# A transformer block on one core: a list scheduler's order against an order written out, operation by operation

## The chip, the cores and the metric

The kernel runs on one core of a Trainium2 chip. Times are device microseconds (us) from the first to the last instruction of an execution, with what lies around it. The kernel before took 836.15 us, the median of three runs (835.84 to 837.64). TensorE (PE in the profile) multiplies matrices, VectorE (DVE) does element-wise work and reductions, ScalarE (ACT) does copies, casts and activations, GpSimd (POOL) a little of the rest, and SyncE (SP) issues nearly all transfers. PEld is the loading of weights into PE, which runs beside its multiplications.

## The reference, cut to what matters

```python
S, D, H, Dh, W, dil, F = 2048, 640, 32, 20, 8, 2, 1728        # all float32, B = 1
def _A_ref(x, wqkv, wo):                                       # attention
    qkv = (x @ wqkv).reshape(B, S, 3, H, Dh) ...               # q, k, v
    idx = pos[:, None] - (arange(W) * dil)[None, :]            # 8 keys: s, s-2, ..., s-14
    logits = einsum("bhsd,bhswd->bhsw", q, k[idx]) * Dh ** -0.5   # masked where idx < 0
    attn = softmax(logits)
    o = einsum("bhsw,bhswd->bhsd", attn, v[idx])
    return o.reshape(B, S, D) @ wo
def _B_ref(x, w_gate, w_up, w_down):                           # feed-forward
    return (silu(x @ w_gate) * (x @ w_up)) @ w_down

h  = x + _A_ref(_layernorm(x), wqkv, wo)
h2 = h + _B_ref(_layernorm(h), w_gate, w_up, w_down)           # the output
```

## The kernel before

Each fp32 matrix product is made of three products of rounded parts: a high part times a high part, a low part times a high part and a high part times a low part. The high part is a cast (on ACT: L506 and L606 for activations, L617 and L939 for weights), the low part the difference between the value and its high part (on DVE: L507, L607, L619, L956). So each tile of activations and of weights goes through ACT and then DVE before PE has all three products.

The sequence is cut into four batches of 512 rows, each of four row groups of 128, and the 640 columns of Q, K and V into four groups of eight heads. For a batch the kernel loads x (L577 row by row for the first batch, L568 in one transfer for another), takes the layer norm on ACT (L382, L389), turns rows into columns (L604 and L504 on PE, or L512, a 128x2560 transpose on DVE), multiplies by the weight tiles of wqkv (loaded by L616, 128x480 each; products L643) and stores Q, K and V in DRAM. The local attention is element-wise work on DVE alone: products with shifted K (L692) and V (L727), sums (L699, L735), maximum and softmax (L710, L711), L765 turns results. Then come the product with wo (L890, evicted by L893), the residual (L901), the second layer norm (L496, L504 to L507 make its columns, high and low part), the products with w_gate and w_up (L962, L1046, L1068), the gating (L986 to L997) and the product with w_down (L973, L1093, L1103, L1298). A part of the feed-forward of the last batches is computed in a form that needs fewer products, by sums and differences of rows: L1204 makes differences of weights, L1207 their low parts, L1223 evicts a product bank into a sum, L1250 multiplies the two halves. That stage runs from about 654 to 766 us and is called the pair stage below. Eight banks of 512 columns take the products, so PE also waits for whoever empties a bank.

The whole program is recorded first: P.add notes the engine, a cost, the tiles read and written and a function for each of 2846 operations. `order()` then puts all of them in one sequence, and each engine's instructions are issued in that sequence. An engine works through its own queue in order: an instruction whose input is not there holds up all that stand behind it on that engine. Before, the sequence comes from a list scheduler (`listed`), which takes the ready operation with the earliest due time; `latest` computes due times backwards from the order of the PE work; nine ROUNDS repeat both with other parameters; and SHIFT moves some 370 operations by hand-set amounts. The costs in P.add, `nb` and HOP are the scheduler's alone.

## Time and profile before

| what | value |
| --- | --- |
| median of the timed runs | 836.15 us (835.84 to 837.64) |
| the profiled execution: span from first to last instruction | 835.3 us |
| PE busy | 826.3 us (99%), 4061 matmuls |
| DVE busy | 755.7 us (90%), 916 instructions |
| ACT busy | 421.3 us (50%), 740 instructions |
| POOL busy | 23.1 us (3%) |
| granted TensorE clock, mean | 0.999 of full speed |
| moved by DMA | 211.08 MB, 253 GB/s on the mean |

The page gives no other time for the profiled execution than its span; the median of the runs is 0.85 us above it. A share of busy time is a mean over the whole span, so the windows below give it by stage. In a timeline, a number in square brackets is the time in which the engine sat idle before the row, and the name behind the arrow is the instruction that ended it. In the chain of waits, "x60" says that 60 instructions of one line ran one behind the other; what they take beyond 60 times the time of one is waiting.

### The profile page before, as it was taken

To read this page: it belongs to the slowest core of one execution; us is meant where nothing else is said; L and a number is where in the kernel's file an instruction comes from. 1 tells how busy PE (TensorE), PEld (TensorE's weight loads), DVE (VectorE), ACT (ScalarE), POOL (GpSimd) and SP (SyncE) were. 2 spreads that over 40 slices of the span, in tenths; PEclk is the share of its full clock that TensorE was granted. 3 is DMA by queue.
4 is the path that set the end of the run, shared out by engine and by line. 5 is a ranking of instruction groups with operands and counts; after the bars stand their busy time and mean duration, and the time that the engine had idled before them with its cause. 6 is when DMAs were issued, how large, how long until landed. Compare 5 with 4: busy or idle time off the path is not lost.

```text
span 835.3 us, 11299 instructions
## 1 busy us (share of the span) xinstructions
PE 826.3 (99%) x4061; PEld 712.8 (85%) x4061; DVE 755.7 (90%) x916; ACT 421.3 (50%) x740; POOL 23.1 (3%) x34
## 2 busy tenths in 40 slices
PE   8999999999999999999999999999999999999998
PEld 6888888889978888887888888888988888888998
DVE  7599999999999999999999999998869888777982
ACT  7856473333783435654543476565695323323440
POOL 0000000000100000001000000000000000000000
PEclk9999999999999999999999999999999999999999
DMA  8897868568679764899899758899999634457722
GB/s 274 288 348 275 267 213 283 185 207 308 186 219 343 257 197 177 326 303 349 282 313 349 271 173 315 255 288 352 352 339 320 224 115 151 124 175 258 273 99 75
DMA packets 113223, 211.08 MB, mean 253 GB/s; under 512 B 37952, under 2 KB 70400, under 8 KB 112528
## 3 DMA queue, kind: packets, MB, share of 16 engines
q1 hardware_dynamic: 112864, 209.96, 74.0%
q8 instruction: 32, 0.52, 0.2%
q10 hardware_dynamic: 304, 0.41, 0.1%
q14 instruction: 23, 0.19, 0.1%
HBM read 151.27 MB, written 59.05 MB: 252 GB/s over the span
## 4 chain that ended last, share of the span: by engine, by line
PE 84%; DVE 8%; ACT 3%; DMA 3%; issue 1%; SPq 0%; POOL 0%; DVEq 0%; ACTq 0%; POOLq 0%
PE bank L962 22%; PE bank L1046 18%; PE bank L643 15%; PE bank L973 10%; PE bank L1298 7%; PE bank L890 6%; DMA fa<-in_x_dram 2%; PE bank L1103 1%; DVE fa L692 1%; PE bank L1093 1%; DVE fa L735 1%; PE bank L1068 1%; DVE fa L727 1%; DVE fa L699 1%; ACT ra L617 1%
## 5 line engine op out<-in xcount | busy, mean ns | idle before, releaser
L962 PE MATMUL bank<-shb,ra 128*128 128x512 f32 x810 | 190.0, 390 | 1.3 <-DVE shb L507 1.3
L962 PEld LDWEIGHTS bank<-shb,ra 128*128 128x128 f32 x810 | 151.4, 188 | 32.7 <-ACT shb L506 1.5
L643 PE MATMUL bank<-ra,sha 128*128 128x480 f32 x480 | 105.2, 379 | 0.2 <-ACT ra L617 0.2
L643 PE MATMUL bank<-ra,shb 128*128 128x480 f32 x470 | 102.5, 378 | 0.0
L643 PEld LDWEIGHTS bank<-ra,sha 128*128 128x128 f32 x480 | 89.8, 188 | 14.5 <-ACT ra L617 0.6
L643 PEld LDWEIGHTS bank<-ra,shb 128*128 128x128 f32 x470 | 88.1, 188 | 13.2
L692 DVE TENSOR_TENSOR fa<-fa 128x2560 f32<-128x2560 f32 x32 | 90.2, 2820 | 0.9 <-DMA fa<-qsc 0.4
L727 DVE TENSOR_TENSOR fa<-fa 128x2560 f32<-128x2560 f32 x32 | 90.3, 2822 | 0.8
L699 DVE TENSOR_REDUCE fa<-fa 128x128 f32<-128x2560 f32 x32 | 89.9, 2810 | 0.4
L1046 PE MATMUL bank<-shb,ra 128*128 128x512 f32 x360 | 89.4, 395 | 0.6 <-DVE fa L990 0.6
L973 PE MATMUL bank<-ra,acts 128*128 128x512 f32 x328 | 80.7, 391 | 0.0
L1046 PEld LDWEIGHTS bank<-shb,ra 128*128 128x128 f32 x360 | 66.0, 188 | 16.2 <-DVE fa L1223 1.7
L735 DVE TENSOR_TENSOR fa<-fa 128x1280 f32<-128x1280 f32 (+2 forms) x70 | 76.7, 1096 | 1.3
L890 PE MATMUL bank<-ra 128*128 128x320 f32 x480 | 74.1, 310 | 0.0
L890 PEld LDWEIGHTS bank<-ra 128*128 128x128 f32 x480 | 71.7, 188 | 2.4 <-ACT fa L893 1.0
L648 ACT ACTIVATE st<-bank,fa 128x480 f32<-128x480 f32 x64 | 41.0, 656 | 64.1 <-PE bank L643 59.5
L973 PEld LDWEIGHTS bank<-ra,acts 128*128 128x128 f32 x328 | 61.1, 188 | 13.2 <-DVE acts L997 0.5
L1046 PE MATMUL bank<-ra 128*128 128x512 f32 x288 | 69.1, 390 | 0.0
L1046 PEld LDWEIGHTS bank<-ra 128*128 128x128 f32 x288 | 53.9, 188 | 11.1
L1223 DVE TENSOR_TENSOR fa<-bank,fa 128x512 f32<-128x512 f32 x60 | 41.0, 689 | 19.8 <-PE bank L1046 19.0
L939 ACT CAST ra<-fa 128x1280 fp32r<-128x1280 f32 (+1 forms) x38 | 45.6, 1207 | 22.9 <-PE bank L962 12.3
L996 ACT CAST acts<-fa 128x512 fp32r<-128x512 f32 x34 | 21.0, 620 | 48.7 <-DVE fa L986 47.0
(189 smaller groups left out, 1059.8 us busy)
## 6 DMA issues: line engine op xcount, KB each, us to landing
fa<-in_ffn_dram SPq DMA_DIRECT2D x28, 960.0 KB, 6.4
fa<-ksc SPq DMA_DIRECT2D x16, 880.0 KB, 5.4
fa<-vsc SPq DMA_DIRECT2D x16, 880.0 KB, 7.3
ra<-lsc SPq DMA_DIRECT2D x21, 640.0 KB, 5.8
ra<-lsc SPq DMA_DIRECT2D x27, 320.0 KB, 3.7
lsc<-ra SPq DMA_DIRECT2D x13, 640.0 KB, 4.6
fa<-in_ffn_dram SPq DMA_DIRECT2D x12, 640.0 KB, 4.0
ra<-tsc SPq DMA_DIRECT2D x8, 960.0 KB, 7.1
```

Source lines behind the costliest of these rows:

```text
L643: T.matmul(banks[bk][:, 0:480], l, r_(wq(g, w, c), 480), start=(p, c) == first_mm, stop=(p, c) == last_mm)
L648: P.add("ACT", act(480) + 0.06, lambda bk=bk, j=j: A.activation(stage_t()[:, so : so + 1920].rearrange("p (t j c) -> p t j c", t=3, j=NJ)[ ...
L692: P.add("DVE", dve(2560), lambda: V.tensor_tensor(f(PROD, 2560).rearrange("p (j w c) -> p j w c", j=2, w=W), window(ko, 2 * jp), f(qo + 32 ...
L699: P.add("DVE", dve(2560), lambda: V.tensor_reduce(f(lo + 128 * jp, 128), f(PROD, 2560).rearrange("p (n d) -> p n d", d=DH), axis=AX.X, op= ...
L727: V.tensor_tensor(f(PROD, 2560).rearrange("p (j w d) -> p j w d", j=2, d=DH), bass.AP(tensor=fa[:, vo : vo + 160].tensor, offset=fa[:, vo ...
L735: V.tensor_add(dst(v), v[:, :, 0:m, :], v[:, :, m : 2 * m, :])
L890: T.matmul(banks[bk][:, 0:320], l, r_(m, 320), start=p == 0 and c == 0, stop=p == 2 and c == NC - 1)
L939: P.add("ACT", act(n), lambda: A.copy(r_(gu, n), f(raw, n)), r=[rf(raw, n)], w=[rr(gu, n)], prio=PR["fh"])
L962: T.matmul(banks[bk], r_(gu + 1280 * w + wid * c + col, 128), x2(a, c), start=p == 0 and c == 0, stop=p == 2 and c == NC - 1)
L973: T.matmul(banks[bk][:, lo:hi], l, m, start=first and p == 0, stop=last and p == len(passes) - 1)
L1046: T.matmul(banks[bk], r_(ws[w] + 256 * q, 128), x(a, c), start=start and p == n == q == 0, stop=stop and p == 2 and n == len(terms) - 1 an ...
L1298: T.matmul(banks[bks[j]][:, 0:320], t(a, 128, 128 * j), r_(ws[w], 320), start=p == q == 0, stop=p == NP - 1 and q == 2)
```

## The change

The list scheduler with its parameters and its SHIFT table goes. In its place stands ORDER, a tuple of all 2846 operation numbers, and `order()` emits the operations by their place in it (an operation comes only after those it depends on). The operations, what they read and write, their shapes and their dependences stay the same; only the sequence differs. Lines of the kernel after are higher by 12 (L604 becomes L616, L616 becomes L628, L1223 becomes L1235).

```diff
-LANES, HOP = 8, 0.035
-LAP = {"PE": 0.0, "ACT": 0.1, "DVE": 0.08, "POOL": 0.0, "SP": 0.0}
-ROUNDS = ((1.1, 3, 3.5), (1.5, 6, 1.5), (1.4, 20, 3.5), ...
-SHIFT = {
-    7: 3.5, 9: -106.8, 22: 0.4, 31: -515.8, 32: -221.5, 33: -238.8, 34: -84.5, 35: -34.6, 36: -483.8, 37:
...
+ORDER = (
+    3, 0, 6, 11, 42, 10, 9, 2, 31, 7, 32, 33, 15, 8, 36, 37, 34, 12, 13, 39, 43, 40, 16, 17, 1, 47, 41, 118, 119, 19,
...
     def order(self):
-        start = self.listed()
-        for stretch, serial, dma in ROUNDS:
-            start = self.listed(self.latest(start, stretch, dma), serial)
...
-        key = [(t + SHIFT.get(n, 0.0), n) for n, t in enumerate(start)]
-        heap, out = [key[n] for n in range(len(ops)) if not left[n]], []
+        place = {n: i for i, n in enumerate(ORDER)}
+        heap, out = [(place.get(n, n), n) for n in range(len(left)) if not left[n]], []
         heapq.heapify(heap)
         while heap:
             n = heapq.heappop(heap)[1]
             out.append(n)
...
-    def latest(self, start, stretch, dma):
...
-    def listed(self, last=None, serial=0.0):
...
```

Of the operations, 642 of PE's 808 stand at another place in its queue than before (164 by more than five places), 753 of DVE's 855 (183 by more than five), 492 of ACT's 579 (100) and 536 of SP's 586 (201, at most 84 places). POOL's 18 stay. Three places follow.

The queue of SP at the start of the program, before: in_x is the first batch's rows (64x640 and 128x640) and the second batch (128x2560), in_wqkv the weight tiles.

```order
L572 DMA fa<-in_x_dram 64x640
L577 DMA fa<-in_x_dram 128x1x640 x3
L616 DMA fa<-in_wqkv_dram 128x480 x8
L349 DMA ksc<-fa 8x1120
L349 DMA vsc<-fa 8x1120
L1411 DMA fa<-in_const_dram 128x1x32
L616 DMA fa<-in_wqkv_dram 128x480 x8
L568 DMA fa<-in_x_dram 128x1x2560
L616 DMA fa<-in_wqkv_dram 128x480 x2
```

The same queue after:

```order
L584 DMA fa<-in_x_dram 64x640
L589 DMA fa<-in_x_dram 128x1x640
L628 DMA fa<-in_wqkv_dram 128x480 x4
L589 DMA fa<-in_x_dram 128x1x640
L628 DMA fa<-in_wqkv_dram 128x480 x2
L589 DMA fa<-in_x_dram 128x1x640
L628 DMA fa<-in_wqkv_dram 128x480 x2
L361 DMA ksc<-fa 8x1120
L628 DMA fa<-in_wqkv_dram 128x480 x7
L580 DMA fa<-in_x_dram 128x1x2560
L628 DMA fa<-in_wqkv_dram 128x480
```

Four weight tiles now go ahead of the last two row loads of the first batch, and 15 instead of 16 stand ahead of the load of the second batch.

The queue of DVE at the first columns of the second layer norm, before: L507 makes the low part of these columns from a bank (bank_73 is the first that PE reads), L496 low parts that come without a bank, L699 is a reduction of the attention, L956 makes low parts of gate and up weights.

```order
L956 TENSOR_TENSOR ra<-fa,ra 128x640
L496 TENSOR_TENSOR shb<-fa,shb 128x2x128 x2
L699 TENSOR_REDUCE fa<-fa 128x128
L710 TENSOR_REDUCE fa<-fa 128x32
L507 TENSOR_TENSOR shb<-bank_73,shb 128x256
L496 TENSOR_TENSOR shb<-fa,shb 128x2x128
L507 TENSOR_TENSOR shb<-bank_74,shb 128x512
L496 TENSOR_TENSOR shb<-fa,shb 128x2x128
L507 TENSOR_TENSOR shb<-bank_75,shb 128x512
```

The same place after (L777 is L765 of before, L519 is L507, L508 is L496, L711 is L699, L968 is L956):

```order
L777 STREAM_TRANSPOSE fa<-fa 128x2x5x32
L722 TENSOR_REDUCE fa<-fa 128x32
L968 TENSOR_TENSOR ra<-fa,ra 128x640
L711 TENSOR_REDUCE fa<-fa 128x128
L508 TENSOR_TENSOR shb<-fa,shb 128x2x128
L968 TENSOR_TENSOR ra<-fa,ra 128x640
L519 TENSOR_TENSOR shb<-bank_74,shb 128x512
L519 TENSOR_TENSOR shb<-bank_73,shb 128x256
L508 TENSOR_TENSOR shb<-fa,shb 128x2x128 x4
L519 TENSOR_TENSOR shb<-bank_75,shb 128x512
```

The bank of 512 columns is now taken first (PE's first product there is also the one that reads it), a transpose L777 stands ahead, and the L508s stand behind the reduction.

The queue of DVE in the pair stage, before: L1223 empties a bank that PE fills next, L1204 and L1207 prepare weights, L1250 is the gating product.

```order
L1250 TENSOR_TENSOR fa<-fa 128x512
L1204 TENSOR_TENSOR fa<-fa 128x512 x3
L1109 TENSOR_TENSOR fa<-bank_72,fa 128x320
L1223 TENSOR_TENSOR fa<-bank_74,fa 128x512
L1207 TENSOR_TENSOR ra<-fa,ra 128x512
L1223 TENSOR_TENSOR fa<-bank_73,fa 128x512
L1207 TENSOR_TENSOR ra<-fa,ra 128x512
L1204 TENSOR_TENSOR fa<-fa 128x512
```

The same place after (L1235 is L1223 of before, L1216 is L1204, L1219 is L1207, L1262 is L1250, L1121 is L1109):

```order
L1235 TENSOR_TENSOR fa<-bank_73,fa 128x512
L1235 TENSOR_TENSOR fa<-bank_75,fa 128x512
L1216 TENSOR_TENSOR fa<-fa 128x512
L1262 TENSOR_TENSOR fa<-fa 128x512
L1121 TENSOR_TENSOR fa<-bank_72,fa 128x320
L1235 TENSOR_TENSOR fa<-bank_74,fa 128x512
L1235 TENSOR_TENSOR fa<-bank_73,fa 128x512
L1219 TENSOR_TENSOR ra<-fa,ra 128x512
L1262 TENSOR_TENSOR fa<-fa 128x512
L1235 TENSOR_TENSOR fa<-bank_73,fa 128x512
```

The evictions L1235 now stand ahead of differences of weights and low parts that stood ahead of them, and come two together.

## Rows read from the trace of the kernel before

**Rows 1.** the page: busy time, then one group of instructions

```profile
PE 826.3 (99%) x4061; PEld 712.8 (85%) x4061; DVE 755.7 (90%) x916; ACT 421.3 (50%) x740; POOL 23.1 (3%) x34
...
L692 DVE TENSOR_TENSOR fa<-fa 128x2560 f32<-128x2560 f32 x32 | 90.2, 2820 | 0.9 <-DMA fa<-qsc 0.4
```

**Rows 2.** windows: length, busy PE, PEld, DVE, ACT, POOL, PEclk, DMA, GB/s

```profile
12.00:34.00 22.00, 22.00 (x103) 19.04 (x102) 12.01 (x35) 17.98 (x45) 0.00 (x0) 1.00 0.89 291
...
39.00:237.00 198.00, 197.84 (x954) 173.46 (x953) 195.00 (x173) 102.36 (x203) 9.05 (x10) 1.00 0.75 246
237.00:242.00 5.00, 3.62 (x20) 2.83 (x19) 5.00 (x10) 4.98 (x8) 0.00 (x0) 1.00 0.91 298
...
654.00:766.00 112.00, 112.00 (x503) 91.99 (x502) 88.52 (x140) 34.77 (x64) 0.10 (x1) 1.00 0.48 160
```

**Rows 3.** waits of PE: line <- what it waited for: us, times, longest

```profile
PE bank L604 <- DVE sha L607: 1.4, 1, 1.4
...
PE bank L962 <- DVE shb L507: 1.3, 1, 1.3
PE bank L1046 <- DVE fa L990: 0.6, 1, 0.6
```

**Rows 4.** waits of all engines, one row of DVE

```profile
DVE fa L512 <- ACT fa L382: 8.5, 1, 8.5
```

**Rows 5.** chain of waits: start us, us, engine and line, instructions

```profile
17.32 10.49 DMA fa<-in_x_dram
...
45.49 4.64 DMA fa<-in_wqkv_dram
...
256.96 6.80 PE bank L962 x30
...
305.93 2.19 PE bank L890 x15
...
308.81 2.29 PE bank L890 x15
...
390.78 4.88 PE bank L973 x19
...
645.78 1.96 PE bank L1093 x12
...
660.97 1.64 PE bank L1046 x6
...
672.25 13.87 PE bank L1046 x60
...
686.84 42.60 PE bank L1046 x186
...
730.17 35.87 PE bank L1046 x156
```

**Rows 6.** timeline of PE at the start: start us, us, instructions, [idle before]

```profile
8.41 0.66 PE L604 MATMUL bank<-fa 128*128 128x128 f32 x4 [1.40 <-DVE sha L607]
...
10.56 0.47 PE L643 MATMUL bank<-ra,sha 128*128 128x480 f32 x1
```

**Rows 7.** timeline of DVE, 35 to 40 us

```profile
38.01 1.19 DVE L619 TENSOR_TENSOR ra<-fa,ra 128x480 fp32r<-128x480 f32 x2
```

**Rows 8.** timeline of DVE around the first LN2 columns

```profile
235.85 2.81 DVE L699 TENSOR_REDUCE fa<-fa 128x128 f32<-128x2560 f32 x1
...
239.10 0.41 DVE L507 TENSOR_TENSOR shb<-bank,shb 128x256 fp32r<-128x256 f32 x1
239.44 0.41 DVE L496 TENSOR_TENSOR shb<-fa,shb 128x256 fp32r<-128x256 f32 x1
239.77 0.68 DVE L507 TENSOR_TENSOR shb<-bank,shb 128x512 fp32r<-128x512 f32 x1
...
243.44 0.90 DVE L765 STREAM_TRANSPOSE fa<-fa 128x320 f32<-128x320 f32 x2
```

**Rows 9.** line L1207: durations ns min/median/max, first and last start

```profile
L1207 DVE TENSOR_TENSOR ra<-fa,ra x24: 679/682/691, 652.1 to 752.2; 128x512 fp32r<-128x512 f32 x24
```

More of the change, by code (lines that the diff above doesn't have):

```diff
@@ L32 @@
 SCALE = DH ** -0.5
[L35 to L37 removed]
 PR = {'tp': 6, 'mx': 2, 'mh': 2, 'ml': 2, 'mld': 3, 'dt': 2.2, 'g1': 0.6, 'y1': 0.6, 'x': 0.5, 'yst': 8, 'yld': 2, 'wqd': 4, 'wqh': 0.5, 'wql': 4, 'qev': 1, 'kvs': 0.4, 'atl': 1.2, 'exp': 0.5, 'ost': 3, 'wod': 2, 'woh': 8, 'wol': 1.2, 'old': 1.5, 'fld': 4, 'lst': 6, 'wev': 1.5, 'fh': 2.2, 'fl': 8, 'ln1': 8, 't1': 1, 'wo0': 1.2, 'wo': 2.2, 'ln1t': 1.2, 'xb': 0.4, 'tr': 10, 't1t': 2.2, 'ln1d': 0.5, 'hst': 10, 'hld': 10, 'ht': 1, 'hc': 2, 'jd': 3, 'jp': 8, 'js': 4, 'jl': 0.4, 'ja': 0.5, 'jfld': 1.2, 'jfh': 4, 'jfl': 1, 'jhi': 4, 'jmu': 0.4, 'jlo': 0.9, 'jcm': 0.5, 'w3': 1, 'w3e': 8, 'w3o': 0.4, 'w3x': 8, 'w3l': 2.2, 'jy': 6}
[L40 removed]
[34 rows of a table removed]
[L75 removed]
+ORDER = (
[143 rows of a table added]
+)
 class Plan:
@@ L102, in order @@
     def order(self):
-        start = self.listed()
-        for stretch, serial, dma in ROUNDS:
-            start = self.listed(self.latest(start, stretch, dma), serial)
-        self.start, self.end = start, max(t + o[1] for t, o in zip(start, self.ops))
-        ops = self.ops
-        left = [len(o[3]) for o in ops]
-        key = [(t + SHIFT.get(n, 0.0), n) for n, t in enumerate(start)]
-        heap, out = [key[n] for n in range(len(ops)) if not left[n]], []
+        left = [len(o[3]) for o in self.ops]
+        succ = [[] for _ in self.ops]
+        for n, o in enumerate(self.ops):
+            for d in o[3]:
+                succ[d].append(n)
+        place = {n: i for i, n in enumerate(ORDER)}
+        heap, out = [(place.get(n, n), n) for n in range(len(left)) if not left[n]], []
         heapq.heapify(heap)
@@ L114, in order @@
             out.append(n)
-            for m in self.succ[n]:
+            for m in succ[n]:
                 left[m] -= 1
                 if not left[m]:
-                    heapq.heappush(heap, key[m])
+                    heapq.heappush(heap, (place.get(m, m), m))
         return out
-    def latest(self, start, stretch, dma):
-        ops = self.ops
-        t, due = 5.0, {}
-        for n in sorted((n for n, o in enumerate(ops) if o[0] == "PE"), key=lambda n: start[n]):
-            due[n] = t
-            t += ops[n][1]
-        last = [0.0] * len(ops)
-        for n in reversed(range(len(ops))):
-            eng, cost, _, _, prio, _, nbytes = ops[n]
-            if eng == "SP":
-                cost += nbytes + dma
-            elif eng == "DVE" and prio == 20:
-                cost *= stretch
-            last[n] = min(min((last[m] - HOP for m in self.succ[n]), default=1e9) - cost, due.get(n, 1e9))
-        return last
```

76 lines of the change are left out of this document (removed), and 175 rows, old and new, of tables (ORDER, SHIFT).

## The prediction

> **What bounds the kernel now.** I read the busy times first: PE works 826.3 us of a span of 835.3, DVE 755.7 [rows 1]. The reader is to see that an order of the same work can win very little: what PE does not use is 9.0 us, and the rest must come from matmuls that are stretched by waits. Next the windows by stage [rows 2], in which two things stand out. From 39 to 237 us DVE has 195.0 busy of 198.0, the pauses between its instructions included, so it is as full as PE there; from 654 to 766 it has 88.52 of 112.0, so it has 23 us of room. And PE loses 1.38 us in the 5 us from 237 to 242. Then who waits for whom: PE has few long waits, 1.4 at the start for L607, 1.3 at L962 for L507 and 0.6 at L1046 for L990 [rows 3]. The longest of DVE is 8.5 us for L382, before it starts its transpose L512 at 35 us [rows 4]; from there on DVE runs without a rest to the wait of PE at 237. So the place at 237 is bound by DVE, not by PE: time that PE wins before it is lost again there, unless DVE comes earlier too. Last the chain of waits, which gives the stretched groups [rows 5]. The measure for these is an undisturbed group: 30 products of 512 columns in 6.80 us, 0.2267 each, and 15 of 320 columns in 2.19 us, 0.146 each.
>
> **The change part by part.** All operations and their durations stay, so each term below is a wait that goes or comes. The sum is made against the profiled execution's 835.3 us; the median of the runs is 836.15, 0.85 above it, and I carry the differences over to the median.
>
> *Start.* SP issues four weight tiles ahead of the second half of the first batch's rows, and PE's first QKV products stand ahead of most L604, where they fill the wait of 1.40 us and come before the 10.56 us at which the first stands now [rows 6]. The gain lies between 0 and 1.4; I take 0.8, near the middle, since one more warm-up product stands first. Another weight tile that is issued at 45.49 and is waited for until about 50.1 [rows 5] is issued some 20 us earlier; that frees at most 0.7 us, taken as 0.65. These 1.45 us of PE count nothing in the sum, because PE arrives earlier at 237 us and there waits for DVE that much longer. If that cover is gone, they are worth 1.45.
>
> *First columns of the second layer norm (237 us).* Between the L512 at 35 us and the first low part, DVE has more ahead of it after: one more L619 (1.19 for two [rows 7], 0.60), one more L765 (0.90 for two [rows 8], 0.45), and the bank of 512 columns, which PE's first product there reads, takes 0.68 where that of 256 took 0.41 (0.27 more); one L496 stands behind it now (0.33, from 239.44 to 239.77 [rows 8]). Together +0.99. Three more L496 stand ahead of the last low part, which adds 1.38 there in all (0.60 + 0.45 + 0.33), but PE has two groups of five products in front of it (2.27), so the first low part decides. Against it stands the second batch's x: it is loaded in 10.49 us from 17.32 [rows 5], and its layer norm is what L512 waits for. One tile of 128x480 (0.246 MB) fewer goes ahead of it; at 291 GB/s [rows 2] that is 0.84. Of the 0.9 us that L692 waits in all, 0.4 is for a load of Q [rows 1], before 237 us; its store and load stand earlier in SP's queue after, and it goes. Net 0.99 - 0.84 - 0.4, about -0.2. The ends: +0.63 if the load takes its 10.49 us from issue whatever is ahead of it, -0.6 if it gains half as much again. I take the middle since the transfers are busy for 22 us on end there, at 0.89 [rows 2].
>
> On this place the row shows a load of 10.49 us, more than twice what its 1.31 MB need at 291 GB/s (4.5), so it stood behind others or shared with them [rows 2, 5]. The Trainium skill, page "DMA: Bandwidth & Descriptors", section "Queues, rings and completion order", says that the transfers of one issuing engine share its rings, one on each DMA engine, and that each consumes its descriptors in ring order. By that rule a tile less ahead is a tile's time less, the -0.2; by the bare row, with a fixed time from issue to landing, it is +0.63.
>
> *Products with wo.* L890 in one bank waits for its eviction where only 0.68 us of other products lie between two groups: 2.29 instead of 2.19 [rows 5], four times. After, 1.4 us or more lie between, and one new pair is as close as before: -0.3. The ends are -0.4 and 0.
>
> *390 us.* 19 products take 4.88 where 19 x 0.2267 = 4.31 [rows 5], because the low part L997 stands behind an L692 of 2.8 us on DVE. After, it stands ahead of it: of 0.57 I take 0.5; the ends are 0.57 and 0.
>
> *565 us.* PE waits 0.6 for L990 [rows 3], which stands behind a 2.8 us L727 in both orders; one L1374 fewer is between the sums and the L727. Between 0 and 0.6 I take 0.35.
>
> *646 us.* 12 products of 320 columns take 1.96 where 12 x 0.146 = 1.75 [rows 5]: -0.2, the ends -0.2 and 0.
>
> *Pair stage.* PE runs into banks that L1223 has not emptied. The groups take 1.64 for 6 (1.36 undisturbed), 13.87 for 60 (13.60), 42.60 for 186 (42.17) and 35.87 for 156 (35.37) [rows 5]: 0.28 + 0.27 + 0.43 + 0.50 = 1.48. After, the evictions stand 3 to 7 us of DVE work further ahead, in a stage in which DVE has room [rows 2], and with the durations of the trace the least margin between an eviction and the product that fills the bank grows from 0.1 to about 2 us, an estimate. A part of the losses has no releaser in the trace, so I take -1.1; the ends are -1.48 and 0.
>
> *New waits.* Of 808 PE operations 642 change place, and not each can come as well covered as before. No row shows them. I take five of 0.1, the size of the wait at L890 [rows 5], +0.5; the ends are 0 and 1.5 (that of the wait at 237, 1.3, and two small ones).
>
> Sum: -0.2 - 0.3 - 0.5 - 0.35 - 0.2 - 1.1 + 0.5 = -2.15, hence 836.15 - 2.15 = 834.0.
>
> **The rivals.**
>
> *The early gains come through.* The second batch's x lands earlier by 1.4 us more than I take, since the whole start of SP's queue is 64 rows and tiles in another order. Then DVE reaches 237 us earlier by that, PE's 1.45 from the start is worth its time, and the result is 834.0 - 1.4 = 832.6. For it speaks that the load takes 10.49 where its bytes need 4.5; against it, that only one tile goes from ahead of it.
>
> *The gains are given back at DVE.* DVE is as full as PE to 237 us [rows 2], and what PE wins at 390 and at the wo products is lost where it next waits for DVE (565 us, L990 behind the L727, which the new order leaves there). Without the 0.3, 0.5 and 0.35, and without the 0.2 at 237, the sum is -0.2 - 1.1 + 0.5 = -0.8, and the result 835.3.
>
> *Slower, by the pair stage.* The evictions stand ahead of the low parts L1207 now. Each product that reads such a low part waits if it comes late, and nothing behind it on PE can go ahead. Its price is one eviction's place, 0.68 us [rows 9], in each of the six pairs, 4.1 us, and the pair stage wins nothing: 834.0 + 1.1 + 4.1 = 839.2. It decides from four pairs on (1.1 + 2.7 = 3.8, 837.8). For it: the 24 low parts now lie behind evictions that wait for PE, so one late bank holds up both. Against: the narrowest of them has a margin of some 1 us in the trace, and by the durations it grows to more than 3, and DVE has 23 us of room.
>
> That the order is not carried out as written is no rival: the engines' queues after are those of ORDER.
>
> **How the numbers follow.** The forecast of 834.0 has a chance of 0.51, the early gains 0.22, gains given back 0.16, slower 0.11. The forecast's own range is 833.2 to 834.9: from 0.8 less (the full 1.48 and no new waits) to 0.9 more (the term at 237 at +0.63). The range for 8 in 10 goes to 831.8, where the early gains come with no new waits (832.6 - 0.5) and a little of the ends beside, and to 836.6, where the gains are given back and the new waits are 1.5 and not 0.5 (835.3 + 1.0, and 0.3 of the ends). What a measurement of this kernel can tell from no change is about 0.2%, 1.67 us; that lies at 834.5 and 837.8. Of the forecast's 0.51 some 0.36 lies below 834.5, with the early gains 0.58 for faster. Its other 0.15 and 0.16 of the gains given back are 0.31 for the same, and the pair stage's 0.11 is slower.
>
> **What would show it.** In the profile after: the first QKV product at about 8 us; the wait of PE for L507's successor L519 about 1.2 us longer than the 1.3 of now (1.45 that PE is earlier, less 0.2 that DVE is); the load of the second batch's x shorter than 10.49 us; no group of L985, the successor of L973, with 4.88 us for 19 near 390 us; in the pair stage no wait for L1235 and PE at less than 1.0 us above the count times 0.2267. I am wrong if the wait at 237 us is gone (then the early gains came through), if PE still waits for L1235, or if it waits for L1219. A change of DVE's 8.5 us wait by more than 1.5 us would overturn the term at 237.

## The result, and the profile after

The changed kernel took 840.91 us (median of 4 runs, 840.04 to 841.76) against 836.0 for the kernel before (4 runs): ratio 1.0048, interval 1.0034 to 1.0062. It is slower; 834.0 was forecast, with 836.6 as the upper end of the range for 8 in 10. Repeated with 10 runs beside 34 of the kernel before (e0 below), the ratio is 1.0034 (1.0023 to 1.0044), 2.9 us. The span of the profiled execution is 839.5 us, 4.2 above before.

The page's busy times, columns as in [rows 1]:

```profile
PE 827.3 (99%) x4061; PEld 713.1 (85%) x4061; DVE 759.1 (90%) x916; ACT 417.3 (50%) x740; POOL 25.1 (3%) x34
```

DVE works 3.4 us more and POOL 2.0 more with the same 916 and 34 instructions. That is the first sign: the durations were to stay. The windows, columns as in [rows 2]:

```profile
12.00:34.00 22.00, 21.08 (x104) 18.01 (x103) 12.99 (x37) 20.23 (x50) 0.00 (x0) 1.00 0.91 291
...
39.00:237.00 198.00, 197.44 (x952) 173.17 (x950) 194.05 (x172) 98.94 (x197) 9.57 (x10) 1.00 0.74 245
237.00:242.00 5.00, 3.25 (x16) 2.53 (x15) 5.00 (x10) 5.00 (x11) 0.00 (x0) 0.83 0.75 231
394.00:565.00 171.00, 169.56 (x791) 141.69 (x789) 167.13 (x166) 90.29 (x140) 7.97 (x8) 1.00 0.87 291
...
654.00:766.00 112.00, 112.00 (x508) 92.26 (x508) 90.89 (x145) 33.79 (x65) 0.10 (x1) 1.00 0.51 169
```

PE now stands still in places where it did not: 0.92 us in 12:34, 1.75 instead of 1.38 in 237:242, and 1.44 in 394:565. The waits of PE, in the form of [rows 3], some of the rows:

```profile
PE bank L974 <- DVE shb L519: 1.2, 1, 1.2
PE bank L616 <- DVE fa L455: 0.9, 1, 0.9
PE bank L985 <- DVE acts L1004: 0.8, 1, 0.8
PE bank L516 <- ACT fa L489: 0.6, 1, 0.6
PE bank L655 <- ACT st L660: 0.6, 1, 0.6
```

The wait for L519, which was to grow to 2.5, is as long as before, and four new ones stand beside it (the one for L489 is scatter at least in part: 0.64 us of it stand in e9 below, whose order there is the old one). The chain in the pair stage, columns as in [rows 5]:

```profile
680.98 10.70 PE bank L1058 x46
692.41 12.07 PE bank L1058 x53
705.21 58.46 PE bank L1058 x255
```

46, 53 and 255 products would take 10.43, 12.02 and 57.83 undisturbed: 0.27, 0.05 and 0.63 are still lost.

To place the loss, take from a product's start the undisturbed times (0.2268 us for 512 columns, 0.2167 for 480, 0.1467 for 320, 0.109 for 128) of all products ahead of it. What is left, less the same 2.2 us in every row for the first products, is the time PE has lost by then:

| at us | 12 | 34 | 100 | 236 | 245 | 387 | 395 | 500 | 560 | 600 | 650 | 760 | last |
| --- | --- | --- | --- | --- | --- | --- | --- | --- | --- | --- | --- | --- | --- |
| before | 4.21 | 4.20 | 4.68 | 4.29 | 6.18 | 6.47 | 7.08 | 7.45 | 7.64 | 8.83 | 9.49 | 10.99 | 10.99 |
| after | 2.84 | 3.93 | 3.72 | 4.34 | 8.15 | 8.61 | 8.60 | 9.87 | 11.60 | 13.14 | 13.42 | 14.54 | 14.74 |
| e0, after again | 2.93 | 4.05 | 3.84 | 5.00 | 7.58 | 8.04 | 8.03 | 8.55 | 10.53 | 11.80 | 12.09 | 13.23 | 13.42 |

The start wins 1.37 us, and at 236 us nothing is left of it. It was not lost in a longer wait at 237, as forecast, but ahead of it: 1.09 between 12 and 34 us, and 0.6 between 100 and 236. Between 236 and 245 us PE then loses 3.81 (e0: 2.58) where it lost 1.89 before, and between 500 and 560 it loses 1.73 (e0: 1.98) where it lost 0.19. The rest of the 4.2 is the way from the last product to the end, about 0.4 longer. The same start scatters by itself: at 12 us the profiles of this document have lost 2.6 to 5.0 with the start of after and 3.7 to 5.9 with that of before, so 1.37 is one pair's figure. In this execution 8 products from 240.5 us took 0.427 us each (the window's granted clock is 0.83, so part of it at 1.2 and not 2.4 GHz), after PE had stood still for 0.75 and 1.32 us.

**What stood still.** DVE and then POOL of the changed kernel, 100 to 108 us, columns as in [rows 8]:

```profile
100.29 2.83 DVE L704 TENSOR_TENSOR fa<-fa 128x2560 f32<-128x2560 f32 x1
103.53 3.82 DVE L541 TENSOR_TENSOR sha<-fa,sha 128x512 fp32r<-128x512 f32 x4 [0.41 <-ACT sha L540]
107.27 2.81 DVE L711 TENSOR_REDUCE fa<-fa 128x128 f32<-128x2560 f32 x1
```

```profile
103.26 0.20 POOL L765 TENSOR_TENSOR fa<-fa 128x1 f32<-128x1 f32 x1 [26.49 <-DVE fa L704]
103.41 1.58 POOL L767 TENSOR_TENSOR fa<-fa 128x640 f32<-128x640 f32 x1
```

The same place in the kernel before:

```profile
104.08 1.89 DVE L529 TENSOR_TENSOR sha<-fa,sha 128x512 fp32r<-128x512 f32 x3
105.89 2.82 DVE L692 TENSOR_TENSOR fa<-fa 128x2560 f32<-128x2560 f32 x1
108.74 2.82 DVE L699 TENSOR_REDUCE fa<-fa 128x128 f32<-128x2560 f32 x1
```

```profile
109.00 1.57 POOL L755 TENSOR_TENSOR fa<-fa 128x640 f32<-128x640 f32 x1
```

POOL adds attention sums as soon as the product L692 is done (its L765 reads one element of the product). In the kernel before, DVE's reduction L699 stands right behind that product in 8 of the 12 places, and behind one other instruction in the other 4; no DVE instruction there is longer than usual. In the new order four L541 stand between. Three would take 1.89 and four 2.5; they take 3.82. The first, alone, took 2.01 instead of 0.68; it ended 0.55 us after POOL's L767, as if it had worked only from there on. The same at 541 us, with an instruction of 128x2 elements (DVE, POOL and ACT):

```profile
541.63 0.16 DVE L469 RECIPROCAL fa<-fa 128x2 f32<-128x2 f32 x1
541.72 1.56 POOL L767 TENSOR_TENSOR fa<-fa 128x640 f32<-128x640 f32 x1
541.82 1.48 DVE L470 TENSOR_TENSOR fa<-fa 128x2 f32<-128x2 f32 x1
543.34 0.16 DVE L471 TENSOR_TENSOR fa<-fa 128x2 f32<-128x2 f32 x1
...
543.73 0.29 ACT L488 ACTIVATE fa<-fa 128x1 f32<-128x1 f32 x1 [3.37 <-DVE fa L472]
```

A third stands at 479 us, the last of three L892, which take 1.80 and not 0.42 for it:

```profile
478.09 3.00 DVE L892 TENSOR_TENSOR ra<-fa,ra 128x512 fp32r<-128x512 f32 x3
```

All that were held read two operands from SBUF; the L1386 at 418 us, with one in a bank, took its usual time beside POOL. The Trainium skill, page "SBUF — State Buffer", section "Who interferes with whom", says that DVE and GpSimd share one pair of ports, that a DVE instruction with two SBUF inputs contends with a GpSimd instruction that reads SBUF, that the order of issue decides which of them waits, and that a reduction never contends. The rows agree: the held ones took 1.3 to 1.4 us more, and the reduction L699 of before took its 2.82 beside L755.

A second wait was not forecast either. DVE at 214 us, and SP ahead of it:

```profile
214.43 0.82 DVE L747 TENSOR_TENSOR fa<-fa 128x640 f32<-128x640 f32 x1 [1.02 <-DMA fa<-qsc]
```

```profile
208.81 0.54 SPq L912 DMA_DIRECT2D fa<-in_x_dram  x1
209.40 0.59 SPq L781 DMA_DIRECT2D osc<-fa  x1
```

The trace names a load of Q. What L747 writes is what the store L781 reads: issued at 209.40, behind a load of x that had waited for DVE, and landed at 214.30. L747 starts 0.13 us after that; in e0, e1 and e6 below it is 0.12 or 0.13 too, and in e0 and e6 the trace names the store itself. e3 and e6 test that.

### The profile page after: what moved, and what is told of

The parts are those of the page before. It is cut to its first block, busy times and chain, and to the rows that moved or that the text cites. A ratio compares the mean times of both kernels' runs of the same rounds, so it can differ in the third digit from the quotient of the medians.

```text
span 839.5 us, 11188 instructions
## 1 busy us (share of the span) xinstructions
PE 827.3 (99%) x4061; PEld 713.1 (85%) x4061; DVE 759.1 (90%) x916; ACT 417.3 (50%) x740; POOL 25.1 (3%) x34
## 4 chain that ended last, share of the span: by engine, by line
PE 63%; DVE 24%; issue 4%; DMA 4%; ACT 4%; SPq 1%; DVEq 0%; ACTq 0%
PE bank L1058 17%; PE bank L974 13%; PE bank L655 11%; PE bank L1310 7%; PE bank L985 5%; PE bank L902 5%; DVE fa L711 5%; DVE fa L739 4%; DVE fa L704 4%; DVE fa L747 3%; DMA fa<-in_ffn_dram 2%; PE bank L1115 1%; PE bank L1105 1%; PE bank L1080 1%; DMA fa<-osc 1%
## 5 line engine op out<-in xcount | busy, mean ns | idle before, releaser
L974 PE MATMUL bank<-shb,ra 128*128 128x512 f32 x810 | 194.5, 392 | 1.6 <-DVE shb L519 1.2
L704 DVE TENSOR_TENSOR fa<-fa 128x2560 f32<-128x2560 f32 x32 | 90.2, 2818 | 0.4
L711 DVE TENSOR_REDUCE fa<-fa 128x128 f32<-128x2560 f32 x32 | 89.8, 2806 | 0.2
L1058 PE MATMUL bank<-shb,ra 128*128 128x512 f32 x360 | 89.5, 393 | 0.3 <-DVE fa L1002 0.3
L985 PE MATMUL bank<-ra,acts 128*128 128x512 f32 x328 | 85.1, 390 | 0.0
L747 DVE TENSOR_TENSOR fa<-fa 128x1280 f32<-128x1280 f32 (+2 forms) x70 | 76.8, 1098 | 2.4 <-DMA fa<-qsc 1.0
L985 PEld LDWEIGHTS bank<-ra,acts 128*128 128x128 f32 x328 | 61.2, 188 | 12.8 <-DVE acts L1004 0.4
L1235 DVE TENSOR_TENSOR fa<-bank,fa 128x512 f32<-128x512 f32 x60 | 40.6, 687 | 18.4 <-PE bank L1058 17.9
L1217 ACT CAST ra<-fa 128x512 fp32r<-128x512 f32 x30 | 17.6, 619 | 51.2 <-PE bank L1058 42.7
```

The costliest lines, as they stand in the source:

```text
L704: P.add("DVE", dve(2560), lambda: V.tensor_tensor(f(PROD, 2560).rearrange("p (j w c) -> p j w c", j=2, w=W), window(ko, 2 * jp), f(qo + 32 ...
L711: P.add("DVE", dve(2560), lambda: V.tensor_reduce(f(lo + 128 * jp, 128), f(PROD, 2560).rearrange("p (n d) -> p n d", d=DH), axis=AX.X, op= ...
L747: V.tensor_add(dst(v), v[:, :, 0:m, :], v[:, :, m : 2 * m, :])
L974: T.matmul(banks[bk], r_(gu + 1280 * w + wid * c + col, 128), x2(a, c), start=p == 0 and c == 0, stop=p == 2 and c == NC - 1)
L985: T.matmul(banks[bk][:, lo:hi], l, m, start=first and p == 0, stop=last and p == len(passes) - 1)
L1058: T.matmul(banks[bk], r_(ws[w] + 256 * q, 128), x(a, c), start=start and p == n == q == 0, stop=stop and p == 2 and n == len(terms) - 1 an ...
```

## The experiments

Two measures are used. The ratio is to the runs of the kernel before on the same chip (its medians there: 837.58, 837.38, 837.05, 836.64, 836.91). The **stretch** is the time from the start of the transpose L524 (L512 before) at 33 to 36 us to the start of the first low part L519 (L507) that PE waits for at 237. L524 starts at 32.6 to 36.7 us in the 20 profiles whatever the order, and DVE carries that to 237; the stretch leaves it out. It scatters as well: in the seven profiles with the order of before from L524 to 237 us (before, e9, e12 to e15, e17) it lies between 203.5 and 205.4. As rows, the kernel before:

```profile
35.25 2.85 DVE L512 STREAM_TRANSPOSE fa<-fa 128x2560 f32<-128x2560 f32 x1 [8.53 <-ACT fa L382]
```

With 239.10 of [rows 8] that is 203.85. The diffs below give DVE's or SP's part of ORDER by operation numbers, and what they are.

| run | ratio to before | interval | stretch |
| --- | --- | --- | --- |
| e0 after again | 1.0034 | 1.0023 to 1.0044 | 206.78 (first profile 206.24) |
| e1 freed at 103 | 1.0031 | 1.0019 to 1.0044 | 205.63 |
| e2 freed at 541 | 1.0015 | 1.0006 to 1.0024 | 206.21 |
| e3 both, and the store | 0.9996 | 0.9988 to 1.0005 | 204.21 |
| e4 before, four behind L704 | 1.0036 | 1.0023 to 1.0049 | 206.67 |
| e5 before, four behind L711 | 1.0036 | 1.0024 to 1.0049 | 208.60 |
| e6 e3 without the store | 1.0005 | 0.9996 to 1.0013 | 204.64 |
| e7 e3, L892, last rows | 0.9997 | 0.9985 to 1.0009 | 204.06 |
| e8 before, two behind L704 | 1.0005 | 0.9997 to 1.0014 | 204.61 |
| e9 before, start of after | 0.9987 | 0.9977 to 0.9996 | 204.71 |
| e10 e3, start of before | 1.0093 | 1.0079 to 1.0108 | 207.30 |
| e11 e10, L892, end of before | 1.0072 | 1.0050 to 1.0093 | 209.47 |
| e12 before, after from 385 | 1.0015 | 1.0006 to 1.0023 | 204.18 |
| e13 e12, start of after | 1.0008 | 0.9998 to 1.0018 | 205.38 |
| e14 e12, held at 541 | 1.0025 | 1.0014 to 1.0036 | 203.87 |
| e15 before, pair stage of after | 0.9999 | 0.9991 to 1.0008 | 203.75 |
| e16 e3, other list | 0.9994 | 0.9983 to 1.0005 | 205.84 (one L892 held) |
| e17 e9, other list | 1.0002 | 0.9992 to 1.0013 | 203.53 |

**e0.** No edit. 

> The changed kernel once more, as the bar for the edits beside it (same order, only the line breaks of the tuple differ). Its profile shows 839.5 us of span against 835.3 before: PE loses 3.75 us more and the tail is 0.4 longer. Two readings of the 8 products from 240.5 us that take 0.427 us each instead of 0.2268 (the granted clock in that window is 0.83): if they belong to the order (PE stood still for 0.75 and 1.32 us just before), they are there again; if they are a chance of that one execution, they are gone and the span is 837.8. In both readings the time is 4 us above the kernel before within 1 us.

The 8 products are at 0.2268 again and the clock is 1.00, though PE stood still for 1.02 and 1.34 us ahead of them. So the lower clock came with one execution, and is not what makes the kernel slower (two of e0's ten runs have a mean granted clock of 0.997 too, the other eight 0.999 or 1.0). Held were one L541 (2.05), the group of L470, and two L892s (1.72 at 194, 1.80 at 479), the first of them here, with POOL beside it:

```profile
194.13 2.53 DVE L892 TENSOR_TENSOR ra<-fa,ra 128x512 fp32r<-128x512 f32 x2
```

```profile
194.82 1.56 POOL L767 TENSOR_TENSOR fa<-fa 128x640 f32<-128x640 f32 x1
```

**e1.**

```diff
-491, 263, 265, 267, 269, 503        (491 L704, 263 to 269 L541, 503 L711)
+265, 267, 491, 503, 269, 263
```

> Changed kernel, with the four L541 behind the L704 at 100 us placed two ahead of it and two behind the reduction L711, so that GpSimd's L767 of 1.58 us lies beside the reduction, as it did before the change. Theory H (a DVE instruction with two inputs in SBUF stands still while GpSimd works: the L541 at 103.5 took 2.01 us instead of 0.68): that L541 takes 0.7, DVE is 1.3 to 1.7 us earlier from 107 to 211 us, and since PE at 237 waits for DVE, its losses from 236 to 245 us (3.8 us: 0.75 + 1.32 of standing still and 1.7 at the lower clock) fall by 1.3 to 3.5; the time falls by 1.3 to 3.5 us. Rival Q (the lead is lost at the next wait anyway, the one of L747 at 214 us, 1.02 us for a DMA): L541 takes 0.7, the wait at 214 grows by the same 1.3 to 2.7, and the time changes by under 0.5 us.

All four L541 take 0.68, and the stretch falls by 1.2, but the wait at 214 grows to 1.36 us and the time by the ratio only from 1.0034 to 1.0031. Both theories were half right: the standing still goes (H), and the time hardly changes (Q). Against e0 the wait at 214 takes back 1.13 us.

**e2.**

```diff
-899, 1709, 1477, 911        (899 L704, 1709 L1009, 1477 L469 to L472, 911 L711)
+1709, 1477, 899, 911
```

> Changed kernel, with the L704 at 538 us behind the five small instructions (L1009, L469 to L472) that stood between it and its reduction. Theory H: the L470 at 541.8 takes 0.16 us and not 1.48, ACT has the deviations 1.3 to 2 us earlier, and PE's losses from 547 to 556 us (1.7 us in the changed kernel) fall by 1.0 to 1.7; the time falls by 1.0 to 1.7 us. Rival (PE there waits for ACT's own queue and for L1004, which are not held): the losses from 547 to 556 stay within 0.4 and so does the time.

L470 takes 0.16 us. PE in 540:556, e0 and then e2:

```profile
540.00:556.00 16.00, 14.89 (x70) 11.55 (x69) 13.98 (x26) 12.45 (x22) 2.02 (x2) 1.00 0.82 275
```

```profile
540.00:556.00 16.00, 15.71 (x75) 12.79 (x74) 14.05 (x23) 11.40 (x21) 1.72 (x2) 1.00 0.86 281
```

PE's loss from 500 to 560 falls from 1.98 to 0.58, the medians from 840.3 to 838.6. H holds, at the upper end.

**e3.** Both edits, and

```diff
-592, 596, 593, 997, 590        (997 L912, the rest L781)
+590, 592, 596, 593, 997
```

> Both edits, and the store L781 of the attention sums at 209.4 us issued first of its group (ahead of a load of x that waits for DVE), which is what L747 waits for at 214 us. Theory H with the wait at 214 taken away too: PE's losses 236 to 245 fall from 3.8 to 0.5 or less, those at 547 to 556 from 1.7 to 0.3, the clock stays up at 240 us, and the time falls by 4 to 5.5 us, to about that of the kernel before or up to 1 us under it. Rival Q (no gain of DVE survives to 237): at most 2 us.

No wait at 214, PE loses 1.20 at 237 (expected at most 0.5; it was 1.89 before), 0.57 between 500 and 560. 837.43 against 840.3 of e0: 2.9 us, less than the 4 to 5.5 expected since 1.7 of the first profile's loss was the clock. DVE's two ends of the stretch in e3:

```profile
34.01 2.85 DVE L524 STREAM_TRANSPOSE fa<-fa 128x2560 f32<-128x2560 f32 x1 [7.33 <-ACT fa L394]
...
238.22 1.02 DVE L519 TENSOR_TENSOR shb<-bank,shb 128x512 fp32r<-128x512 f32 x2
```

204.21. So three small edits of the sequence take the ratio back to 1 within its interval. Not all is freed: the L892 at 479 us is still held (1.79 us) in e3, and in every kernel here with that part of the new order. And the kernel before runs at a lower clock more often than e3 does, which the paragraph on the granted clock below takes up.

**e4 and e5,** in the order of the kernel before.

```diff
-263, 265, 490, 267, 269, 271, 491, 503        (490 L747, 271 L541)
+490, 271, 491, 263, 265, 267, 269, 503        (e4)
+490, 271, 491, 503, 263, 265, 267, 269        (e5)
```

> The order of the kernel before, written out as a tuple, with one edit: the four L541 (L529 of before) at 102 us go behind the L704 (L692) and ahead of its reduction, which is what the changed kernel does. Theory H: one of the four takes 2.0 us and not 0.68, DVE is 1.3 us late from there to 237 us, where PE waits for it, and the loss of PE from 236 to 245 us grows from 1.9 to 3.2: time +1.0 to +1.5 us. Rival S (what hurts in the changed kernel is the sequence on DVE as such, so late low parts, not the standing still): all four take 0.7, time within 0.4 us of before.

> The same four instructions moved one place further, behind the reduction, so that they come even later than in e4 but no two-input instruction stands beside GpSimd's work. Theory H: all take 0.7 and the time is that of the kernel before within 0.4 us, so 1.0 to 1.5 less than e4. Rival S: if the later low parts hurt, this one is as slow as e4 or slower.

In e4 one L541 takes 2.06 us:

```profile
105.58 3.86 DVE L541 TENSOR_TENSOR sha<-fa,sha 128x512 fp32r<-128x512 f32 x4
```

Yet e5, with none held, is as slow. DVE waits 3.11 us at 115 for L394 there, because ACT's layer norm stands behind the last L541, and PE 1.8 us at 157, behind which the clock fell for 8 products. And in both the L541 that stands right behind L747 now waits (1.26 and 0.84 us). So e5 is no control for e4: Rival S is right that late low parts cost too, and e4 may hold both prices at once; these two runs do not part them.

**e6.** e3 without the third edit. 

> e3 without the store L781 moved ahead: the changed kernel with both groups of held instructions freed. Theory H with the store as a second, separate wait: L747 waits 1.0 to 1.4 us at 214 us as in e1, PE's loss from 236 to 245 us is about 2.6 and not e3's 1.2, and the time is 1.0 to 1.5 us above e3 (that is, about e2). Rival (the store was not what L747 waited for, and e3's gain there came from the freed instructions): as fast as e3 within 0.4 us and no wait at 214.

L747 waits 0.44, the stretch is 0.43 longer than e3's; the ratios differ by 0.0009, which their intervals do not tell apart. The store is what L747 waits for, at 0.44 us in this execution and 1.36 in e1; what it is worth in time is not resolved.

**e7.** e3, with 949 (an L892) ahead of 587 (L704) and the last rows as before. 

> e3, with one of the two L892 at 194 us moved ahead of its L704 (in two of the executions the second of them took 1.7 and 1.8 us instead of 0.42), and the last four rows of the output added and stored in the sequence of the kernel before. Theory H: no held instruction before 237 us; the end of the last product to the end of the span falls from 4.5 to 4.1 us; the time is 0.4 to 0.8 below e3, so about 0.1% below the kernel before. Rival (the output stores at the end only vary from run to run): as e3.

As e3. From the last product's start to the end of the span it is still 4.5 us (4.2 before): the sequence of these last rows alone does not make it; e11 says more.

**e8.**

```diff
-267, 269, 271, 491, 503
+267, 491, 269, 271, 503
```

> Order of the kernel before, with only the last two of the L541 at 105 us moved behind the next L704, ahead of its reduction. (In e4 an L747 had also moved, and an L541 then waited 1.26 us for ACT.) Measured from the start of the transpose L524 at 33 to 35 us to the first low part L519 that PE waits for at 237 us, which leaves out the scatter of the start: 204.3 us in the kernel before. Theory H: one L541 takes 2.0 us, this stretch is 205.5 to 205.9, the time +1.0 to +1.5. Rival (the extra duration lies beside a wait that DVE has anyway): the stretch stays within 0.4 of 204.3.

To the end of the first low part the stretch is 205.02, 0.8 above before; 0.58 of that is a wait at 52 us. No L541 was held. DVE and POOL:

```profile
106.85 1.29 DVE L541 TENSOR_TENSOR sha<-fa,sha 128x512 fp32r<-128x512 f32 x2
```

```profile
107.08 1.11 POOL L765 TENSOR_TENSOR fa<-fa 128x1 f32<-128x1 f32 x1 [28.33 <-DVE fa L704]
108.15 1.57 POOL L767 TENSOR_TENSOR fa<-fa 128x640 f32<-128x640 f32 x1
```

It was POOL that stood still: its L765 took 1.11 instead of 0.20, and its long L767 came beside the reduction. H as I had put it was too simple: who begins first goes on, and the other pays. The two L892 behind the product at 194 us show it, with the same DVE queue at that place. Where DVE ran through without a pause (after, e1, e3, e6, e10), neither was held, and POOL's L767 took 1.75 or 1.76 instead of 1.57. Where DVE paused between them (0.14 us in e0, 0.02 in e2, 0.07 in e16), L767 began before the second or with it, and that took 1.72 to 1.84. Where three or more instructions stood behind the product, one was held in every profile.

**e9.** The order of before, what begins before 34 us there in the order of after. 

> Order of the kernel before, with only what begins before 34 us in the order of the change, on all engines. The prediction's reading: the load of the second batch's x is 0.8 us shorter, L524 starts 0.8 earlier, PE's gain at the start is lost at 237 us: -0.5 to -0.8. Theory X, from the traces of e0 to e7: the rows 2 and 3 of the first batch land at 10 and 12 us instead of 6.7 and 7.7, their buffer is free later and the load of x is issued at 18.2 to 20.4 us instead of 16.8 to 17.3, and that eats what it saves: L524 starts at 33 to 35.6 as before, time within 0.7 of before.

0.13% faster, clear of 1 by 0.0004. PE loses 2.60 to 34 us and not 4.20, and 5.81 to 245, not 6.18. Theory X misses too: the load of x was issued at 16.48 here and not at 18 to 20. A difference from after stands in a row. DVE of after, and then of e9, where the queues are the same:

```profile
10.66 0.65 DVE L631 TENSOR_TENSOR ra<-fa,ra 128x480 fp32r<-128x480 f32 x1
12.62 0.29 DVE L619 TENSOR_TENSOR sha<-bank,sha 128x128 fp32r<-128x128 f32 x1 [1.31 <-PE bank L616]
```

```profile
10.53 0.65 DVE L631 TENSOR_TENSOR ra<-fa,ra 128x480 fp32r<-128x480 f32 x1
11.09 0.29 DVE L619 TENSOR_TENSOR sha<-bank,sha 128x128 fp32r<-128x128 f32 x1
```

L619 (operation 49) reads columns of a bank that operation 62, an L616, doesn't write. But a wait is set for the whole bank, by the place in the one list: ORDER of after has 62 ahead of 49, the list that I had built for e9 has it behind. The layer norm L455 behind L619 is late by as much, and it is what PE's L616 waits for at 14 us. e16 takes this wait out of e3, e17 puts it into e9.

**e10 and e11.** e3 with what begins before 34 us in the order of before; e11 also the end and the L892. 

> e3 with everything that begins before 34 us in the order of the kernel before. Theory X: L524 starts as in the kernel before (33 to 35), PE loses 4.2 us to 34 us and not 4.7, and the time is that of e3 within 0.7. If the change's start costs by delaying the load of x (stronger form of X), 0.7 to 1.5 less than e3; if the change's start is worth its early products, 0.7 to 1.4 more.

> e10, with one L892 at 194 us ahead of its L704 as in e7 and everything that begins after 780 us in the order of the kernel before. The stretch from the start of the last product to the end of the span is 4.5 us in the changed kernel and 4.2 before, also in e7 with only the last rows moved. If the order of the last 50 us makes that, it is 4.2 here and the time is 0.3 below e10; if it is scatter, 4.5 and no difference. The best version that these runs point to: 0.1 to 0.2% below the kernel before.

Both fail as tests. At the seam PE waits for ACT in a place that neither whole order has:

```profile
PE bank L655 <- ACT st L660: 2.6, 1, 2.6
```

In e11 the clock also fell after it (0.40 us a product of 480 columns at 44.4 to 47.6 us, not 0.2167), in e10 it did not. What the old start is worth in e3 they do not tell. But e11 answers its other question: from the last product's start to the end it has 4.22 us, e10 4.39. All eight profiles with the order of before at the end have 4.21 to 4.23, the twelve with that of after (e7's last rows aside) 4.38 to 4.67. So the order behind 780 us makes the longer end.

**e12 and e14.** e12: before to 385 us, then after with e2's edit; e14 the same without that edit. 

> The order of the kernel before for all that begins before 385 us there, and the order of the change from there on, with the held instructions at 541 us freed as in e2. The prediction's terms for 390, 565, 646 us and the pair stage are -0.5, -0.35, -0.2 and -1.1: -2.15 together. The traces of e0 to e7 put them at -0.3, -0.5, -0.3 and -0.4, and show +0.4 at 547 to 556, +0.6 at 577 to 600 and +0.3 at the end: -0.2. So 835 by the prediction, 837 by the traces, where the kernel before is at 837.2.

> e12 with the L704 at 538 us put back ahead of the five small instructions, as the change has it. Theory H: an instruction of 128x2 elements takes 1.48 us and not 0.16 while GpSimd's L767 lies beside it, PE loses 1.0 to 1.7 us more between 547 and 556 us, and the time is 1.0 to 1.7 above e12. Rival (e2's gain came from what else the change moves before 385): within 0.4 of e12.

e12 pays 1.46 us at the seam (L985 for L1004 at 395). The forecast's 0.5 at 390 is in it: from 387 to 440 us PE loses 0.18 beside the 1.46, before 0.67. From 440 to the end it is 3.42, before 3.85. So the second half is worth at most 0.9, not 2.15, ahead of a longer end. e14, one line away, in 540:556, beside e12:

```profile
540.00:556.00 16.00, 14.85 (x69) 11.55 (x68) 14.06 (x24) 12.45 (x22) 0.00 (x0) 1.00 0.82 264
```

```profile
540.00:556.00 16.00, 15.72 (x75) 12.77 (x74) 14.05 (x23) 11.54 (x21) 1.73 (x2) 1.00 0.85 284
```

L470 takes 1.48 again and PE loses 1.3 us more (1.89 against 0.60 from 500 to 560). The times go the same way, 838.42 against 837.9, but these two intervals overlap, and the runs of the two with a granted clock of 0.999 or more have the same median (837.69 and 837.73, 5 and 4 runs); e2 against e0 has the price in time.

**e13.** e12 with the start of after. 

> e12 with the start (before 34 us) of the change, too. If e9's 1.2 us are the start's own, it comes through and this is 1.0 to 1.5 below e12, and about 0.15% or more below the kernel before. If e9 was scatter, as e12 within 0.4.

0.6 us below e12 by the ratio, with the same median (837.92 and 837.90), not resolved: in its profiled execution PE waited 1.8 us at 53.7 for an L631.

**e15.** Before, with 600 to 780 us of after. 

> The order of the kernel before, with the order of the change between 600 and 780 us alone (the pair stage and a little ahead of it). The prediction's term: -1.1 and -0.2. By the traces: no wait of PE for L1235 any more, but only 0.4 of the 1.5 us that PE loses there gone. So 835.9 by the prediction, 836.8 by the traces, where the kernel before is at 837.2.

0.9999: the forecast's -1.3 us (0.9984) lies outside the interval. PE loses 1.32 from 650 us to the last product, before 1.50.

**e16 and e17.** e3 and e9 with another list and, on every engine, the same queue.

```diff
-62, 25, 26, 142, 59, 28, 73, 49        (e16)
+25, 26, 28, 73, 49, 62, 142, 59
-49, 50, 75, 97, 120, ..., 141, 62, 142        (e17)
+120, ..., 141, 62, 49, 50, 75, 97, 142
```

> The kernel of e3 (after, with the three edits that take back the meetings of DVE with GpSimd) with one line of the list moved: operation 49 (DVE L619, bank_73) stands ahead of operation 62 (PE L616, same bank). Every engine's own queue is the same as in e3; only the waits change: L619 waits for ACT and no longer for PE's L616, and L616 now waits for L619. Theory L (the one list sets the waits as well as the queues): L619's wait of 1.31 us at 11 us goes, PE's loss of about 1.1 us at 14.6 us goes, the load of the second batch's x is issued about 1.3 us earlier, and the time is 0.8 to 1.4 us below e3's, 0.998 to 0.999 of before. Rival: PE's loss at the start is made up by what waits for x at 237 us, and the time stays within 0.4 us of e3's, 0.9991 to 1.0005 of before.

> The kernel of e9 (before, with the start of after alone) with one line of the list moved: operation 62 (PE L616) stands ahead of operation 49 (DVE L619), as in after. Every engine's queue is the same as in e9. Theory L: L619 waits for L616 again (about 1.3 us), PE loses about 1.1 us at 14.6 us, and the time rises by 0.8 to 1.4 us from e9's 0.9987, to 0.9995 to 1.0005 of before. Rival (the gain of e9 has nothing to do with this wait): as e9, 0.998 to 0.9992.

The same DVE row in e16, in e17, and what PE waits for in e17:

```profile
12.20 0.28 DVE L619 TENSOR_TENSOR sha<-bank,sha 128x128 fp32r<-128x128 f32 x1
```

```profile
13.20 0.29 DVE L619 TENSOR_TENSOR sha<-bank,sha 128x128 fp32r<-128x128 f32 x1 [1.22 <-PE bank L616]
```

```profile
PE bank L616 <- DVE fa L455: 0.9, 1, 0.9
```

So the list alone makes and unmakes the wait, and PE's 1.1 us at 14 us with it (e16 has none, e17 1.08). The time doesn't follow as theory L had it: e16 is where its rival put it, 0.2 us from e3 by the ratio. In its profile x was issued 1.0 us earlier than in e3, and its layer norm began 0.5 later; DVE's L524 came at 34.50, not 34.01, and at 237 PE waited again. e17 has the value of theory L, but its interval overlaps that of e9, and in its own profile PE loses less to 245 us (5.00) than in e9. So the 0.13% of e9 these ratios don't tie to this wait, and with 18 intervals of 95% one that ends 0.0004 below 1 may be chance.

**The granted clock of the runs.** Each timed run has its mean granted clock on record, and it goes with the start. Of the 211 runs of kernels that start in the order of before (139 of them of the kernel before itself), 121 have 0.998 or less; of the 116 that start in the order of after, 11. The kernel before takes 837.2 to 838.2 us in such runs (medians of its five sets of runs) and 835.9 to 836.4 in the others. The profiles of e8, e11 and e12 (old start) show where: the granted clock is 0.81, 0.81 and 0.73 from 9 to 11 us and 0.55, 0.50 and 0.61 from 11 to 14, so part of the time it is the lower of the two levels, after PE had stood still for 1.4 to 2.0 us at about 7 us. Before, e14 and e15 have a pause of 1.4 us there and keep 1.00, and of the eleven profiles with the new start only e7 falls (0.50 from 9 to 11 us). So part of what the new start wins is a clock that falls less often, which the prediction does not have. Why it does is not shown.

The ratios above mix this in. With runs of 0.999 or more alone, on the same chip, the medians stand above the kernel before by 3.8 us in e0 (8 runs), 2.2 in e2, 1.5 in e6, 1.0 in e3, 0.4 in e16 and 1.3 in e17, and 0.5 below in e9. So the three edits take away about 2.8 us of 3.8, and what makes e3 level with the kernel before is, by these numbers, that its clock falls less often. About half of e9's gain is the clock. And the wait of L619 would be worth 0.7 us (e16 against e3) and 1.8 (e17 against e9), which speaks for theory L; as these comparisons were chosen after the results and the chips of each pair differ, that is not shown.

## Why the prediction was wrong

*The step that failed* is "New waits ... I take five of 0.1, +0.5; the ends are 0 and 1.5", together with the claim that all operations keep their durations. Three DVE instructions of after do not, and four of e0: each took 1.3 to 1.4 us more. With two of them freed and the store moved, 2.9 us are won back (e3 against e0; e2 alone 1.7). Of the 3.8 us that e0 takes more than the kernel before at the same clock, 1.0 stays in e3; 0.4 of that lies in the longer end, the rest is open. DVE and POOL were in the trace of before: the L755 at 109.00 lay beside an L699. I read the moves of DVE by what they put ahead of PE's waits, and not by what they put between L692 and L699. The rows in the section on the change do not show it either; POOL's queue was the one that I took as unmoved. Of the three signs of being wrong that the prediction named, none came: the wait at 237 us stayed, and none stood for L1235 or L1219.

*237 us.* The arithmetic of DVE's work was right: it gave +0.99 to the end of the first low part, which is +0.72 to its start since the bank of 512 columns comes first, and -0.4 for the wait of L692, hence 203.85 + 0.3 = 204.2; e3 has 204.21, e7 204.06. As one order's stretch scatters by up to 1.9, so close a fit is luck in part. What the forecast lacked lies on top: up to 2.6 us of held instructions and store in e0. The -0.84 for the load of x did not come. From issue to the first layer norm it takes 7.4 to 8.0 us in the eight profiles that have the change's start and the wait of L619, against 8.4 to 10.5 in eight with the old start (e11 aside, where it came at 29.3); but it is issued at 18.2 to 20.4, not 16.8 to 18.1, and the layer norm begins at 26.6 us on the mean of either. Without that wait (e9, e13, e16) it is issued at 16.5 to 18.0, takes 8.5 to 9.1, and the layer norm begins at 26.2 on the mean, hardly earlier. So neither of my two ends (a fixed 10.49 from issue, a tile's time less) is right: here the landing hardly followed the issue. The 8.5 us wait of DVE came out at 7.1, within the bound that I had set.

*Start.* The 0.8 was 1.37 at 12 us; 1.08 of it went at 14.6 us, by the wait of L619. "The engines' queues after are those of ORDER" was true and not enough: the list sets the waits as well, and I had not read them. By the ratio it costs little, as e16 shows: the 1.0 us that PE is ahead of e3 at 34 us are gone at 100, so they too are not lost at 237, as the prediction had it. What the start does to the clock, in the paragraph above, the prediction did not have.

*wo, 390, 565, 646 us.* Right in sign, as losses of PE: -0.2 (300 to 318 us), -0.3 (385 to 398), -0.54 (560 to 575) and -0.2 (640 to 650), against -0.3, -0.5, -0.35, -0.2. What is won at 565 is lost again by 600: from 575 to 600 us PE loses 0.97 in after, 0.71 in e0 and 0.23 in e3, where it lost 0.08, among other things in a wait for ACT's L905 that was not there.

*Pair stage.* Mis-sized: -0.2 of -1.1 (from 650 us to the last product PE loses 1.32 in after, 1.50 before; e15 has 1.32 with this part alone). That PE runs into full banks was a reading of the chain, and no row bears it out: PE is busy for 112.00 of the 112.00 us of 654:766 in both kernels, and the trace has no wait of PE there for an eviction. With the evictions moved ahead, most of the loss is still there; what it is stays open.

*The rivals.* "Slower, by the pair stage" had the sign, and the wrong mechanism: no L1219 was waited for. "Gains given back at DVE" is nearest to e3 (835.3 forecast, 0.9996 of before measured).

The ends of the forecast's own range are 0.88 and 0.83 away by its terms, where it says 0.8 and 0.9; that changes nothing.

What else is open: which of the operations behind 780 us make the end 0.3 to 0.4 us longer, and how much of e9's gain is real. None of the versions tried beats the kernel before beyond doubt; e9 is the nearest to it.

## What to carry to other kernels

When an order moves, look at pairs of engines that share something, not only at queues: here, what DVE does while GpSimd works. A sum or a search with fixed durations doesn't hold such a price, so an order must be read against the trace for it. Read the waits of an order written out by hand too: one list for all engines sets them, and the same queues can wait differently. Where one engine is full for a long stretch, measure the stretch itself, from its first to its last instruction; it leaves out the scatter of the start, though it still moved by 0.5 us between two profiles of one kernel (206.24, 206.78). And compare the granted clock of the runs as well as their times: here it falls in more than half of the runs of one order and in a tenth of the other's, and that is worth 1.2 to 2.3 us.

## What the runs showed of the hardware

A DVE instruction of 128x2 elements took 1.48 us instead of 0.16 beside a GpSimd addition of 1.56, and a GpSimd instruction of one element took 1.11 instead of 0.20 behind two of DVE. The granted clock fell to its lower level after pauses of 0.75 and 1.32 us in one execution and not in the next, which had 1.02 and 1.34; after 2.77 us it fell in e11 and not in e10. The mean granted clock of a run was 0.998 or less in 121 of 211 runs with the one start and in 11 of 116 with the other; in three profiles of the former it was 0.50 to 0.61 from 11 to 14 us.
